# Gated linear attention and max-out MoE on one core: weights w2 and w_out loaded ahead of unit 0, w1 ahead of unit 1, unit 2 loaded by halves

## The chip, the core and the metric

The kernel runs on one core of a Trainium2 chip. The time is the device time of one launch in microseconds (us). It is the median of several executions; the profile comes from one further execution and is read beside its own time.

## What is computed

```python
def _attn_ref(q, k, v, alpha):                    # (4, 8, 768, 48) each
    B, H, S, D = q.shape
    state = np.zeros((B, H, D, D), dtype=np.float32)
    y = np.zeros_like(q)
    for t in range(S):
        state = alpha[:, :, t, :, None] * state + np.einsum('bhd,bhe->bhde', k[:, :, t], v[:, :, t])
        y[:, :, t] = np.einsum('bhd,bhde->bhe', q[:, :, t], state)
    return y

def _moe_ref(x, w1, w2, w_out):                   # x (3072, 384), w1, w2 (384, 1024), w_out (1024, 384)
    h1 = x @ w1
    h2 = x @ w2
    g = np.maximum(h1, h2)
    return g @ w_out

x = np.ascontiguousarray(attn_out.transpose(0, 2, 1, 3)).reshape(B * S, H * D)
out = _moe_ref(x, w1, w2, w_out)
```

A recurrent attention with a decay alpha per step, head and channel, and then a layer that takes the larger of two projections and projects back. Inputs and output are float32; the kernel multiplies in float16.

## The kernel before

**Units.** The sequence of 768 is cut into 6 chunks of 128 steps, the batch of 4 into 2 groups of two. A unit is one chunk of one group: 12 units, 0 to 11, with unit u chunk u // 2 of group u % 2. Inside a unit, `bb` is 0 or 1, one half for each of the two batch entries. The state goes from unit u - 2 to unit u, so units 0 and 1 have none to take in.

**What one unit does.** `ln(u)`: logarithm of alpha, on ACT. `sums(u)`: prefix sums of it by matmuls, on PE. `exps(u)`: five exponentials on ACT (Em and cs for each half, then the decay de). `kmul(u, bb)` on POOL and `qmul(u, bb)` on DVE scale k and q; `vcast` on POOL casts v to float16; `scale(u, bb)` is these three. `turn(u, bb)`: transposes of k and q on PE, copied as qk by DVE. `kv`: the chunk's own contribution to the state, matmuls and DVE copies or additions into tm. `pairs(u, bb)`: the 128x128 products of q and k, which DVE masks into pt, two instructions a half. Then the attention output: for units 0 and 1 `yfirst` and `xfirst` by halves (matmul, ACT copy xn, transposes, DVE copy xt), for later units `ystate`, `yin` and `xturn`.

**The MoE.** max(x w1, x w2) is computed as relu(x (w1 - w2)) + x w2. `wsub(n)` forms a quarter of w1 - w2 on DVE; `hid(u, f2)`, f2 = 0 to 3, multiplies x by it and takes the relu (ACT for f2 = 0, 1, 2, DVE for 3) into gT; `outp(u, n)` multiplies gT by w_out and adds x times the product w2 w_out. That product w2o is made once: `wturn(ds)` transposes w2, `wcast(n)` casts half of w_out (ACT and POOL), `wmul(n)` multiplies, `wout()` copies the three results out of PSUM.

**Order.** The schedule is manual: each engine runs its instructions in the order in which the program calls these functions, and the semaphores between them are put in by the framework. All input loads are issued on the SP queue in program order; a unit's loads are alpha (two DMAs) and k, q, v (one DMA each for both halves, or one for each half). The framework hands eight DMA semaphores round, so that a DMA is issued after an earlier one on the same semaphore, as a rule the eighth before it, has landed. Outputs are issued on the ACT queue. The load buffers (`ldp`, 4 deep) hold four units.

**The head.** Lines 424 to 508 write out units 0 and 1, the preparation of the weights and the start of unit 2 by hand; `dummies(n)` issues n matmuls whose result is not used. From `for u in range(2, NU)` on, a loop runs the remaining units, with MoE u - 1 among the steps of unit u and the scaling of unit u + 1. Before, the head in order: loads of unit 0's alpha and first half, w2, unit 0's second half, w_out, alpha of unit 1, w1, the rest of unit 1; unit 0 runs while w2 is turned; the product w2 w_out comes after unit 0's second half; then `wsub` and MoE 0 (`hid(0, *)`) among the scaling of unit 1, and MoE 1 with only scaling and `turn` of unit 2.

**PSUM.** Buffers by tag: "g" (4 buffers) for sums, transposes and attention, "pp" (2) for pairs, "m" (2) for hid, outp, the w2 transposes and the dummies; the product w2 w_out uses both pp buffers and one g buffer until `wout`.

Of the kernel before, what the change touches and what calls it, by code (L numbers as in the profile page):

```python
# [15 lines left out]
def kernel(  # L16
# [22 lines left out]
    nc = tc.nc  # L39
# [23 lines left out]
    def load_alpha(u):  # L63
        c, g = divmod(u, NG)
        t = st.setdefault(u, {})
        t["af"] = ldp.tile([128, H, 2, D], FP32, tag="af", name="af")
        for bb in range(2):
            nc.sync.dma_start(  # L68
                out=t["af"][64 * bb : 64 * bb + 64],
                in_=alpha[2 * g + bb, :, c * C : (c + 1) * C, :].rearrange("h (p j) d -> p h (j d)", j=2),  # L70
            )

    def load_kqv(u, bbs):
        c, g = divmod(u, NG)
        t = st[u]
        for name, src in (("kf", k), ("qf", q), ("vf", v)):
            if name not in t:
                t[name] = ldp.tile([128, 2, H, D], FP32, tag=name, name=name)
            lo, hi = bbs[0], bbs[-1] + 1
            nc.sync.dma_start(  # L80
                out=t[name][:, lo:hi].rearrange("p b h d -> p (b h) d"),
                in_=src[2 * g + lo : 2 * g + hi, :, c * C : (c + 1) * C, :].rearrange("b h p d -> p (b h) d"),
            )

    def load(u):
        load_alpha(u)
        load_kqv(u, (0, 1))
# [1 line left out]
    w2f = wp.tile([128, ND, DFF], FP32)  # L89
    wof = wp.tile([128, NF, DM], FP32)  # L90
    w1f = wp.tile([128, ND, DFF], FP32)
    load_alpha(0)
    load_kqv(0, (0,))
    for ds in range(ND):
        nc.sync.dma_start(out=w2f[:, ds], in_=moe_w2[ds * 128 : (ds + 1) * 128])
    load_kqv(0, (1,))
    for n in range(2):
        f = slice(n * NF // 2, (n + 1) * NF // 2)
        nc.sync.dma_start(out=wof[:, f], in_=moe_w_out.rearrange("(s p) d -> p s d", p=128)[:, f])
    load_alpha(1)  # L100
    for n in range(4):
        f = slice(n * DFF // 4, (n + 1) * DFF // 4)
        nc.sync.dma_start(out=w1f[:, :, f], in_=moe_w1.rearrange("(s p) f -> p s f", p=128)[:, :, f])  # L103
    load_kqv(1, (0,))
    load_kqv(1, (1,))

    wz = constp.tile([128, 512], FP16)
    nc.vector.memset(wz, 0.0)
# [48 lines left out]
    def ln(u):  # L157
        X = st[u]
        X["lg"] = LG[u % NB]
        nc.scalar.activation(  # L160
            out=X["lg"][:, :, :, 0:D], in_=X["af"].rearrange("p h j d -> p j h d"), func=ACTF.Ln
        )
# [8 lines left out]
    def sums(u):  # L171
        X = st[u]
        c, g = divmod(u, NG)
        lg = X["lg"]
        cs = [new("g", [128, 512], FP32, 4, "cs") for _ in range(2)]
        X["csv"] = csv = [x[:, 0 : H * D].rearrange("p (h d) -> p h d", h=H) for x in cs]
        dps = cs[0][:, H * D : H * D + 4 * HP].rearrange("p (j b n) -> p j b n", j=HP, b=2)
        for hp in range(HP):
            for j in range(2):
                nc.tensor.matmul(  # L180
                    dps[:, hp], lhsT=pair(lg[:, j], hp), rhs=halves, start=(j == 0), stop=(j == 1)
                )
        for j in range(2):
            for bb in range(2):
                r = slice(64 * bb, 64 * bb + 64)
                nc.tensor.matmul(csv[bb], lhsT=mc[r, j], rhs=lg[r, j, :, 0:D], start=(j == 0), stop=(j == 1))  # L186
        X["dps"] = dps
        X["qn"], X["kn"], X["Em"] = [], [], []
        for bb in range(2):
            X["qn"].append(QN[(2 * u + bb) % (2 * NB)])  # L190
            X["kn"].append(KN[(2 * u + bb) % (2 * NB)])
# [17 lines left out]
    def exps(u):  # L209
        for bb in range(2):  # L210
            expm(u, bb)
            expp(u, bb)
        expd(u)
# [57 lines left out]
    def pairs(u, bb):  # L271
        X = st[u]
        qk = X["qk", bb]
        pt = X["pt", bb] = gp.tile([128, 2, HP, C], FP16, tag="pt", name="pt")
        pa = [new("pp", [128, HP, C], FP32, 2, "pp") for _ in range(2)]
        for j in range(HP):
            for a in range(2):
                r = slice(64 * a, 64 * a + D)
                nc.tensor.matmul(pa[a][:, j, :], lhsT=qk[r, 1, j, :], rhs=qk[r, 0, j, :], start=True, stop=True)  # L279
        for a in range(2):  # L280
            nc.vector.tensor_mul(out=pt[:, a], in0=pa[a], in1=u16.unsqueeze(1).to_broadcast([128, HP, C]))  # L281
# [40 lines left out]
    def yfirst(u, bb):  # L322

        X = st[u]
        ya = new("g", [128, H, D], FP32, 4, "yb")
        for h in range(H):
            nc.tensor.matmul(
                ya[:, h, :], lhsT=X["pt", bb][:, h % 2, h // 2, :], rhs=X["v16"][:, bb, h, :], start=True, stop=True
            )
        if bb == 0:  # L330
            X["xn"] = gp.tile([128, 2, HP, 2, D], FP16, tag="xn", name="xn")
            X["xt"] = mp.tile([128, ND, 2, C], FP16, tag="xt", bufs=3, name="xt")
        nc.scalar.copy(out=X["xn"][:, bb].rearrange("p j a d -> p (j a) d"), in_=ya)

    def xfirst(u, bb):
        X = st[u]
        xp = new("g", [128, ND, C], FP16, 4, "xb")
        xf = X["xn"][:, bb].rearrange("p j a d -> p (j a d)")
        for ds in range(ND):
            nc.tensor.transpose(xp[:, ds, :], xf[:, ds * 128 : (ds + 1) * 128], ident)  # L340
        nc.vector.tensor_copy(out=X["xt"][:, :, bb, :], in_=xp)
# [38 lines left out]
    def wturn(ds):  # L380
        wt = new("m", [128, NF, 128], FP16, 2, "wt")
        for f in range(NF):
            nc.tensor.transpose(wt[:, f, :], w2h[:, ds, f * 128 : (f + 1) * 128], ident)
        nc.vector.tensor_copy(out=w2T[:, :, ds * 128 : (ds + 1) * 128], in_=wt)
# [13 lines left out]

    def wout():
        for ds in range(ND):  # L400
            nc.scalar.copy(out=w2o[:, ds, :], in_=wqs[ds])

    def wcast(n):
        nc.scalar.copy(out=wo16[:, 4 * n : 4 * n + 2], in_=wof[:, 4 * n : 4 * n + 2])
        nc.gpsimd.tensor_copy(out=wo16[:, 4 * n + 2 : 4 * n + 4], in_=wof[:, 4 * n + 2 : 4 * n + 4])
# [7 lines left out]
    def dummies(n):  # L413
        warm = new("m", [128, 512], FP32, 2, "warm")
        for _ in range(n):
            nc.tensor.matmul(warm, lhsT=wz[:, 0:128], rhs=wz, start=True, stop=True)  # L416
# [5 lines left out]


    dummies(10)
    ln(0)
    sums(0)
    exps(0)
    dummies(6)
    scale(0, 0)
    for ds in range(ND):  # L430
        nc.scalar.copy(out=w2h[:, ds, :], in_=w2f[:, ds, :])
    turn(0, 0)
    kv(0, (0,))
    dummies(2)
    pairs(0, 0)
    dummies(2)
    wturn(0)
    yfirst(0, 0)
    dummies(2)
    wturn(1)  # L440
    dummies(2)
    xfirst(0, 0)
    wturn(2)
    scale(0, 1)
    dummies(2)
    turn(0, 1)
    kv(0, (1,))
    dummies(3)
    pairs(0, 1)
    load(2)  # L450
    dummies(6)
    wcast(0)
    yfirst(0, 1)
    wmul(0)
    xfirst(0, 1)
    wcast(1)
    wmul(1)
    ln(1)
    wout()

    sums(1)
    load(3)
    wsub(0)
    wsub(1)
    hid(0, 0)
    expm(1, 0)
    hid(0, 1)
    expp(1, 0)
    wsub(2)
    wsub(3)  # L470
    hid(0, 2)
    expm(1, 1)
    expp(1, 1)
    scale(1, 0)
    hid(0, 3)
    expd(1)
    turn(1, 0)
    kv(1, (0,))
    outp(0, 0)
    scale(1, 1)  # L480
    pairs(1, 0)
    load(4)
    turn(1, 1)
    kv(1, (1,))
    yfirst(1, 0)
    outp(0, 1)
    pairs(1, 1)
    ln(2)
    xfirst(1, 0)
    sums(2)  # L490
    dummies(2)
    yfirst(1, 1)
    exps(2)
    dummies(2)
    xfirst(1, 1)
    for bb in range(2):
        kmul(2, bb)
    state(2)
    vcast(2)
    for bb in range(2):  # L500
        qmul(2, bb)
    hid(1, 0)
    hid(1, 1)
    turn(2, 0)
    hid(1, 2)
    turn(2, 1)
    hid(1, 3)
    load(5)


    for u in range(2, NU):
        nxt = u + 1 < NU
        pairs(u, 0)
        kv(u)
        if nxt:
            ln(u + 1)
        if u > 2:
            hid(u - 1, 0)
            hid(u - 1, 1)
        else:  # L520
            outp(1, 0)
        if nxt:
            sums(u + 1)
            exps(u + 1)
            for bb in range(2):
                kmul(u + 1, bb)
            state(u + 1)
            vcast(u + 1)
        pairs(u, 1)
        if u > 2:  # L530
            hid(u - 1, 2)
        ystate(u)
        if u > 2:
            hid(u - 1, 3)
        if nxt:
            for bb in range(2):
                qmul(u + 1, bb)
        yin(u)
        outp(u - 1, 0 if u > 2 else 1)
        if nxt:  # L540
            turn(u + 1, 0)
        xturn(u)
        if nxt:
            turn(u + 1, 1)
        if u > 2:
            outp(u - 1, 1)
        if u + 4 < NU:
            load(u + 4)
# [34 lines left out]
```

## Time and profile before

| what | us |
|---|---|
| median of 13 runs | 155.21 |
| lowest, highest | 154.23, 157.5 |
| the profiled execution's own time | 155.68 |
| its span, first to last instruction | 154.0 |
| PE busy, share of the span | 140.9 (92%) |
| DVE, ACT, POOL busy | 93.2, 78.7, 47.5 |
| mean rate of all DMA | 186 GB/s, 28.58 MB |
| mean granted clock of PE | 0.986 |

The profiled execution is 0.47 us longer than the median. PE, DVE, ACT and POOL are the matmul, vector, scalar and GpSimd engines; PEld is the weight load of PE. SP only issues DMAs. A busy PE is a modelled end of pipelined matmuls. In a timeline row, "idle before" is the time for which that engine had nothing running, and the name behind it is the instruction or DMA whose semaphore came last. A wait that is put down to an engine can be one for something older.

### The profile page before, as it was taken

How to read it: one execution, taken by the hardware profiler on the slowest of the kernel's cores; microseconds unless marked ns; L12 is line 12 of the kernel's file. 1: busy time of each engine (PE TensorE's matmuls, PEld its weight loads, DVE VectorE, ACT ScalarE, POOL GpSimd, SP SyncE). 2: the span in 40 equal slices, each digit the busy share in tenths (PEclk: the TensorE clock that was granted, in tenths of full speed). 3: DMA queues.
4: the chain of work that ended last, by engine and by line, in shares of the span. 5: the costliest groups of instructions: out<-in, count | busy, mean ns of one | idle time of the engine just before them, and what ended most of it. 6: DMA issues, size and time to landing. Idle time of an engine off the chain costs nothing.

```text
span 154.0 us, 4086 instructions
## 1 busy us (share of the span) xinstructions
PE 140.9 (92%) x1671; PEld 96.7 (63%) x1671; DVE 93.2 (61%) x192; ACT 78.7 (51%) x165; POOL 47.5 (31%) x73
## 2 busy tenths in 40 slices
PE   6878898777799899999999999999999999999991
PEld 2236354344376687777777777777767767767660
DVE  5057816675259699495786775866858575753010
ACT  3365137712563668285392762944918629244421
POOL 6032320330080717227054090360721805400000
PEclk9999999999779999999999999999999999999998
DMA  3999999999999799999999999999998952020202
GB/s 82 199 381 218 366 229 321 172 206 171 236 201 185 155 198 219 196 231 223 168 261 189 236 206 194 238 187 196 234 185 193 235 100 98 4 102 4 97 5 102
DMA packets 93459, 28.58 MB, mean 186 GB/s; under 512 B 87424, under 2 KB 93056, under 8 KB 93440
## 3 DMA queue, kind: packets, MB, share of 16 engines
q1 hardware_dynamic: 90160, 23.60, 85.1%
q10 hardware_dynamic: 3280, 4.72, 8.6%
q8 instruction: 13, 0.21, 0.7%
q14 instruction: 6, 0.05, 0.1%
HBM read 23.59 MB, written 4.72 MB: 184 GB/s over the span
## 4 chain that ended last, share of the span: by engine, by line
PE 70%; SPq 18%; DMA 3%; ACT 3%; issue 2%; ACTq 1%; DVE 1%; POOL 0%
PE op L370 19%; PE hp L352 19%; SPq L80 10%; PE op L368 8%; PE tp L243 6%; SPq L103 4%; PE pp L279 4%; DMA vf<-in_v_dram 3%; PE cs L186 3%; PE kv L259 3%; PE ya L303 3%; PE xp L318 2%; SPq L68 2%; PE ya L291 2%; PE cs L180 1%
## 5 line engine op out<-in xcount | busy, mean ns | idle before, releaser
L232 POOL TENSOR_TENSOR kn<-kf,Em 128x384 f16<-128x384 f32 x24 | 23.5, 998 | 74.8 <-ACT Em L197 63.0
L352 PE MATMUL hp<-xt,w 128*128 128x256 f16 x288 | 38.2, 276 | 1.9 <-DVE w L409 1.2
L281 DVE TENSOR_TENSOR pt<-pp,u 128x512 f16<-128x512 f32 x48 | 30.9, 686 | 13.4 <-PE pp L279 13.0
L370 PE MATMUL op<-wo,gT 128*128 128x384 f16 x192 | 35.1, 326 | 0.0
L373 ACT COPY outs<-op 128x384 f32<-128x384 f32 x24 | 11.5, 479 | 42.8 <-PE op L370 42.8
L352 PEld LDWEIGHTS <-w 128*128 128x128 f16 x288 | 26.1, 99 | 8.0 <-DVE w L409 2.4
L370 PEld LDWEIGHTS <-gT 128*128 128x128 f16 x192 | 18.8, 98 | 12.4
L245 DVE COPY qk<-tp 128x1024 f16<-128x1024 f16 x24 | 16.5, 687 | 12.5 <-PE tp L243 12.5
L357 ACT ACTIVATE gT<-hp 128x512 f16<-128x512 f32 x36 | 20.6, 594 | 5.3 <-PE hp L352 4.9
L236 DVE TENSOR_TENSOR qn<-qf,cs 128x384 f16<-128x384 f32 x24 | 12.3, 548 | 7.9 <-ACT de L207 6.5
L368 PE MATMUL op<-w2o,xt 128*128 128x384 f16 x72 | 15.6, 325 | 0.0
L160 ACT ACTIVATE lg<-af 128x768 f16<-128x768 f32 x12 | 10.1, 842 | 9.7 <-DMA af<-in_alpha_dram 5.5
L416 PE MATMUL warm<-wz 128*128 128x512 f16 x39 | 12.8, 458 | 1.3 <-DVE halves L123 1.3
L359 DVE TENSOR_SCALAR gT<-hp 128x512 f16<-128x512 f32 x12 | 8.3, 691 | 8.2 <-PE hp L352 8.2
L197 ACT ACTIVATE Em<-cs 128x384 f32<-128x384 f32 x24 | 11.7, 488 | 1.1 <-PE cs L186 1.1
L202 ACT ACTIVATE cs<-cs 128x384 f32<-128x384 f32 x24 | 11.8, 491 | 0.0
L169 POOL CAST v<-vf 128x768 f16<-128x768 f32 (+1 forms) x14 | 10.3, 733 | 4.4 <-DMA vf<-in_v_dram 4.4
L267 DVE TENSOR_TENSOR tm<-kv,sb 64x192 f32<-64x192 f32 x32 | 11.3, 353 | 0.5
L243 PE MATMUL tp<-ident,qn 128*128 128x128 f16 x96 | 9.3, 219 | 1.1 <-DVE qn L236 1.0
L279 PEld LDWEIGHTS <-qk 48*128 48x128 f16 x192 | 6.2, 94 | 6.1 <-issue 3.1
L243 PE MATMUL tp<-ident,kn 128*128 128x128 f16 x96 | 9.3, 219 | 0.5 <-POOL kn L232 0.5
L279 PE MATMUL pp<-qk 48*128 48x128 f16 x192 | 9.5, 217 | 0.2 <-DVE qk L245 0.2
(57 smaller groups left out, 143.3 us busy)
## 6 DMA issues: line engine op xcount, KB each, us to landing
af<-in_alpha_dram SPq DMA_DIRECT2D x24, 192.0 KB, 5.7
out_dram<-outs ACTq DMA_DIRECT2D x11, 384.0 KB, 4.2
kf<-in_k_dram SPq DMA_DIRECT2D x10, 384.0 KB, 6.3
qf<-in_q_dram SPq DMA_DIRECT2D x10, 384.0 KB, 7.5
vf<-in_v_dram SPq DMA_DIRECT2D x10, 384.0 KB, 7.0
w2f<-in_moe_w_dram SPq DMA_DIRECT2D x3, 512.0 KB, 5.2
wof<-in_moe_w_out_dram SPq DMA_DIRECT2D x2, 768.0 KB, 7.2
w1f<-in_moe_w_dram SPq DMA_DIRECT2D x4, 384.0 KB, 8.5
```

What stands on the lines that cost most here:

```text
L80: nc.sync.dma_start(out=t[name][:, lo:hi].rearrange("p b h d -> p (b h) d"), in_=src[2 * g + lo : 2 * g + hi, :, c * C : (c + 1) * C, :].r ...
L232: nc.gpsimd.tensor_mul(out=X["kn"][bb][:, :, 0:D], in0=X["kf"][:, bb], in1=X["Em"][bb])
L236: nc.vector.tensor_mul(out=X["qn"][bb][:, :, 0:D], in0=X["qf"][:, bb], in1=X["csv"][bb])
L243: nc.tensor.transpose(tp[:, n, j, :], pair(src, j), ident)
L245: nc.vector.tensor_copy(out=qk, in_=tp)
L279: nc.tensor.matmul(pa[a][:, j, :], lhsT=qk[r, 1, j, :], rhs=qk[r, 0, j, :], start=True, stop=True)
L281: nc.vector.tensor_mul(out=pt[:, a], in0=pa[a], in1=u16.unsqueeze(1).to_broadcast([128, HP, C]))
L352: nc.tensor.matmul(hp[:, n, :], lhsT=w12[:, ds, f * 128 : (f + 1) * 128], rhs=X["xt"][:, ds].rearrange("p n t -> p (n t)"), start=(ds == 0 ...
L357: nc.scalar.activation(out=gT[:, 2 * f2 : 2 * f2 + 2, :], in_=hp, func=ACTF.Relu)
L368: nc.tensor.matmul(op, lhsT=X["xt"][:, ds, n, :], rhs=w2o[:, ds, :], start=(ds == 0), stop=False)
L370: nc.tensor.matmul(op, lhsT=X["gT"][:, f, n * C : (n + 1) * C], rhs=wo16[:, f, :], start=False, stop=(f == NF - 1))
L416: nc.tensor.matmul(warm, lhsT=wz[:, 0:128], rhs=wz, start=True, stop=True)
```

## The change

The loads at the top are put in another order: w2, w_out, all of unit 0 (by halves), w1, then units 1 and 2, both by halves; `load(2)` in the head goes. `wout` moves from ACT to DVE. In the head the preparation of w2 and w_out stands ahead of unit 0; the `wsub` quarters stand in unit 0's second half and MoE 0; `ln`, `sums` and `exps` of unit 1 follow MoE 0's relus; `yfirst(1, 1)` comes ahead of `sums(2)`; unit 2's `vcast` is split, and its first `pairs`, its second `qmul` and its `kv` stand inside MoE 1. Dummies are placed anew, 39 in all before and after. The loop is the same but for unit 2's `pairs(u, 0)` and `kv(u)`, which it leaves out.

```diff
--- before.py
+++ after.py
@@ -89,20 +89,21 @@
     w2f = wp.tile([128, ND, DFF], FP32)
     wof = wp.tile([128, NF, DM], FP32)
     w1f = wp.tile([128, ND, DFF], FP32)
-    load_alpha(0)
-    load_kqv(0, (0,))
     for ds in range(ND):
         nc.sync.dma_start(out=w2f[:, ds], in_=moe_w2[ds * 128 : (ds + 1) * 128])
-    load_kqv(0, (1,))
     for n in range(2):
         f = slice(n * NF // 2, (n + 1) * NF // 2)
         nc.sync.dma_start(out=wof[:, f], in_=moe_w_out.rearrange("(s p) d -> p s d", p=128)[:, f])
-    load_alpha(1)
+    load_alpha(0)
+    load_kqv(0, (0,))
+    load_kqv(0, (1,))
     for n in range(4):
         f = slice(n * DFF // 4, (n + 1) * DFF // 4)
         nc.sync.dma_start(out=w1f[:, :, f], in_=moe_w1.rearrange("(s p) f -> p s f", p=128)[:, :, f])
-    load_kqv(1, (0,))
-    load_kqv(1, (1,))
+    for u in (1, 2):
+        load_alpha(u)
+        load_kqv(u, (0,))
+        load_kqv(u, (1,))
 
     wz = constp.tile([128, 512], FP16)
     nc.vector.memset(wz, 0.0)
@@ -398,7 +399,7 @@
 
     def wout():
         for ds in range(ND):
-            nc.scalar.copy(out=w2o[:, ds, :], in_=wqs[ds])
+            nc.vector.tensor_copy(out=w2o[:, ds, :], in_=wqs[ds])
 
     def wcast(n):
         nc.scalar.copy(out=wo16[:, 4 * n : 4 * n + 2], in_=wof[:, 4 * n : 4 * n + 2])
@@ -422,96 +423,91 @@
 
 
     dummies(10)
+    for ds in range(ND):
+        nc.scalar.copy(out=w2h[:, ds, :], in_=w2f[:, ds, :])
+        wturn(ds)
+        dummies(2)
+    wcast(0)
+    wmul(0)
+    wcast(1)
+    wmul(1)
     ln(0)
     sums(0)
+    wout()
     exps(0)
-    dummies(6)
+    dummies(4)
     scale(0, 0)
-    for ds in range(ND):
-        nc.scalar.copy(out=w2h[:, ds, :], in_=w2f[:, ds, :])
     turn(0, 0)
     kv(0, (0,))
     dummies(2)
     pairs(0, 0)
-    dummies(2)
-    wturn(0)
-    yfirst(0, 0)
-    dummies(2)
-    wturn(1)
-    dummies(2)
-    xfirst(0, 0)
-    wturn(2)
     scale(0, 1)
     dummies(2)
     turn(0, 1)
     kv(0, (1,))
+    yfirst(0, 0)
+    dummies(2)
+    pairs(0, 1)
+    xfirst(0, 0)
+    wsub(0)
+    dummies(5)
+    yfirst(0, 1)
+    wsub(1)
     dummies(3)
-    pairs(0, 1)
-    load(2)
-    dummies(6)
-    wcast(0)
-    yfirst(0, 1)
-    wmul(0)
     xfirst(0, 1)
-    wcast(1)
-    wmul(1)
+
+    load(3)
+    hid(0, 0)
+    wsub(2)
+    hid(0, 1)
+    wsub(3)
     ln(1)
-    wout()
-
+    hid(0, 2)
+    hid(0, 3)
     sums(1)
-    load(3)
-    wsub(0)
-    wsub(1)
-    hid(0, 0)
-    expm(1, 0)
-    hid(0, 1)
-    expp(1, 0)
-    wsub(2)
-    wsub(3)
-    hid(0, 2)
-    expm(1, 1)
-    expp(1, 1)
+    exps(1)
+    outp(0, 0)
     scale(1, 0)
-    hid(0, 3)
-    expd(1)
     turn(1, 0)
     kv(1, (0,))
-    outp(0, 0)
+    outp(0, 1)
     scale(1, 1)
     pairs(1, 0)
     load(4)
     turn(1, 1)
     kv(1, (1,))
     yfirst(1, 0)
-    outp(0, 1)
     pairs(1, 1)
     ln(2)
     xfirst(1, 0)
+    dummies(3)
+    yfirst(1, 1)
     sums(2)
-    dummies(2)
-    yfirst(1, 1)
     exps(2)
     dummies(2)
     xfirst(1, 1)
     for bb in range(2):
         kmul(2, bb)
+        vcast(2, (bb,))
     state(2)
-    vcast(2)
-    for bb in range(2):
-        qmul(2, bb)
+    qmul(2, 0)
     hid(1, 0)
     hid(1, 1)
     turn(2, 0)
     hid(1, 2)
+    pairs(2, 0)
+    qmul(2, 1)
     turn(2, 1)
     hid(1, 3)
+    kv(2)
     load(5)
 
 
     for u in range(2, NU):
         nxt = u + 1 < NU
-        pairs(u, 0)
-        kv(u)
+        if u > 2:
+            pairs(u, 0)
+            kv(u)
         if nxt:
             ln(u + 1)
         if u > 2:
```

## The prediction

> **What bounds the kernel now.** I read the page's slices first. From slice 12 (46 us) on the matmul engine is 9 or more tenths busy; later periods are 10.07 us apart (the 12 matmuls of hp start at 55.66, 65.71, 75.78 us) and hold almost no gap. The change ends before that loop, so what counts is when its steady part begins. Before it the DMA row is full while PE is not, and the chain of waits is nearly all SP queue up to 29 us.
>
> ```profile
> PE   6878898777799899999999999999999999999991
> DMA  3999999999999799999999999999998952020202
> GB/s 82 199 381 218 366 229 321 172 206 171 236 201 185 155 198 219 196 231 223 168 261 189 236 206 194 238 187 196 234 185 193 235 100 98 4 102 4 97 5 102
> ```
>
> Next the timeline of the head: who starts at which landing. Columns: start, duration, engine, line, tiles, and in brackets the idle time and who ended it.
>
> ```profile
> 5.40 0.84 ACT L160 ACTIVATE lg<-af 128x768 f16<-128x768 f32 x1 [3.32 <-DMA af<-in_alpha_dram]
> 9.85 1.05 ACT L431 CAST w2h<-w2f 128x1024 f16<-128x1024 f32 x1 [0.96 <-DMA w2f<-in_moe_w_dram]
> 12.59 1.05 ACT L431 CAST w2h<-w2f 128x1024 f16<-128x1024 f32 x1 [0.42 <-DMA w2f<-in_moe_w_dram]
> 15.49 0.50 POOL L169 CAST v<-vf 128x384 f16<-128x384 f32 x1 [0.73 <-DMA vf<-in_v_dram]
> 18.53 0.83 ACT L404 CAST wo<-wof 128x768 f16<-128x768 f32 x1 [4.52 <-DMA wof<-in_moe_w_out_dram]
> 21.21 0.83 ACT L404 CAST wo<-wof 128x768 f16<-128x768 f32 x1 [0.98 <-DMA wof<-in_moe_w_out_dram]
> 23.34 0.84 ACT L160 ACTIVATE lg<-af 128x768 f16<-128x768 f32 x1 [1.30 <-DMA af<-in_alpha_dram]
> 25.33 0.83 PE L352 MATMUL hp<-xt,w 128*128 128x256 f16 x6 [0.31 <-DVE w L409]
> 34.45 0.51 POOL L169 CAST v<-vf 128x384 f16<-128x384 f32 x1 [2.00 <-DMA vf<-in_v_dram]
> 42.63 2.07 PE L352 MATMUL hp<-xt,w 128*128 128x256 f16 x12 [0.45 <-DVE xt L341]
> 47.52 0.65 PE L368 MATMUL op<-w2o,xt 128*128 128x384 f16 x3
> ```
>
> Each bracket is a landing: unit 0's alpha at 5.4, w2 done at 12.6, unit 0 done at 15.5, w_out at 18.5 and 21.2, unit 1's alpha 23.3, w1 24.3 to 27.7, unit 1's last v 34.4. MoE 0 begins at 25.33, MoE 1 at 42.63, and outp(1,0), from which on both kernels do the same, at 47.52. Last the granted clock in stretches of 3.41 us (columns: stretch, its length, PE busy, matmuls, clock, DMA share, GB/s):
>
> ```profile
> 26.83:30.24 3.41, 2.42 (x20) 1.00 1.01 169
> 33.65:37.07 3.42, 2.41 (x30) 1.00 1.08 154
> 37.07:40.48 3.41, 2.01 (x27) 1.00 0.99 177
> 40.48:43.89 3.41, 2.96 (x21) 0.50 1.22 289
> ```
>
> A stretch with 2.01 us of matmul is followed by one at half clock, one with 2.41 is not. Half clock cost 1.0 us here: two dummies took 1.03 us where others take 0.59 (0.4 more), and 12 hp matmuls 2.07 where they take 1.47 (0.6).
>
> **The change, step by step.** The bytes are the same; the order is new. I walk it from start to outp(1,0), with durations from these rows.
>
> *Loads.* Alpha 0 (two transfers) was in at 5.40, kqv transfers are 1.0 apart, so the first w2 piece, of 1.4 (9.85 to 12.59 is two), lands at 5.4 - 2 x 1.0 + 1.4 = 4.8, the third at 7.6. A w_out half: by the landings 2.9 ((21.21 - 15.49) / 2); by the rate in the slices that held large packets (366 to 381 GB/s, 786 KB) 2.1. I take 2.4: 10.0 and 12.4; ends 11.8 and 13.3. Alpha 0 follows 2.1 later (21.21 to 23.34): 14.5. Unit 0's six kqv, 1.05 each, end at 20.8, w1 (4 x 1.2) at 25.5, alpha 1 at 27.6, the time at which w1 ended before; unit 1 lands as before, up to 34.4.
>
> *w2 and w_out.* Casts 1.05 and transposes follow each landing. wcast(1) 0.83 after 12.4, wmul(1) 2.11: 15.4. ln(0) is behind the casts on ACT, ends 14.5 + 0.84 = 15.3; sums(0) is behind wmul(1) on PE: 15.4 (ends 14.6, 16.2). Before, sums(0) was at 6.30: this 9.1 us is what moving it past w2 and w_out costs.
>
> *wout on DVE.* No row has this copy. Bounds: 0.36 (128x384 f16 from PSUM, L341) and 0.69 (128x512 f32, L359); 0.5, three 1.5, in place of 1.22 on ACT. DVE has nothing to do from 15.4 until qmul(0,0) at 18.0, so nothing; without that cover all 1.5 would delay unit 0. The Trainium skill ("Advanced Engine Details and Errata", The Read-Write Bubble) says ScalarE is nearer to PSUM, VectorE to SBUF; by that rule the move loses, by the rows 0.3 us, under cover either way.
>
> *Unit 0.* sums(0) to the end of pt(0,0) took 6.30 to 12.61 = 6.3: 21.7. In DVE's order qmul(0,1) stands behind it (0.5: 22.2), then q's transposes and the qk copy (1.2, as 16.18 to 17.36: 23.4), tm 0.6, the two pt 1.3: 25.3; xt(0,0) 0.3: 25.6. wsub(0) and wsub(1) (1.99 for two) stand ahead of xt(0,1): 27.5, then 0.35 more, and MoE 0 starts at 27.8, against 25.33: 2.5 late. xfirst(0,1) alone would be in by 26.8 (pt 25.3, yb 0.4, xn 0.5, xb 0.35, dummies beside them), so the wsubs cost 0.6 of it.
>
> *MoE 0, unit 1.* w1 is there: the waits of 0.2 to 0.4 before each hp group go, the buffers set the pace. hp to relu 0.87 + 0.60: hid(0,2) at 29.3, hid(0,3) 29.95; ln(1) 0.84 lies between relus, sums(1) 30.7, Em 31.55, de ends 1.76 later (7.12 to 8.88): 33.3. qmul 0.55, transposes, kv: 34.4; outp(0,1) 1.8: 36.2; pairs(1,0) 0.4, its pt 1.3: 37.85; qk(1,1) 0.6, tm 0.7: 39.1; pt(1,1) 1.25: 40.3. Nothing waits for unit 1's v (34.4) any more. yfirst(1,1) now stands ahead of sums(2): 40.7; xn 0.5, sums(2), two dummies and xb: 42.0; xt 0.4. MoE 1 at 42.45, against 42.63. So 2.3 of the 2.5 us come back. exps(2) ends at 43.1.
>
> *Unit 2 in MoE 1.* qmul(2,0) 43.7, hid(1,0) and (1,1) 1.31: 43.75; transposes 0.45; hid(1,2) 0.65; qk copied at 44.9; pairs(2,0) 45.0 to 45.35; pt(2,0) 1.3: 46.65. qmul(2,1) is now behind pt(2,0) on DVE: 47.15. turn(2,1) is ahead of hid(1,3) and kv(2) on PE and needs it, so PE stands from 45.5 to 47.2: a new wait of 1.65, with all of PE behind it. Then 0.2 + 0.65 + 0.45: outp(1,0) at 48.55, against 47.52. **Sum: 1.05 later.** In exchange pairs(2,0) and kv(2) are done, but before they also were by 47.52.
>
> *The rest, at nothing.* SP issues six halves for unit 2, where there were three: 3 x 0.6 us of SP, under landings of 1 us each. load(3) waits for the DMA eight earlier on its semaphores, now out 0 (issued about 37, landed 5 us later), so alpha 3 lands up to 1.5 later than before; ln(3) had it before 46.3 and sums(3) needs it at 50.4. If that cover went, at most the rest of 1.5 shows. vcast(2) in two casts costs POOL 2 x 0.50 - 0.82, in a POOL idle 69% of the span. Same dummies in all (39).
>
> *The clock.* With the stall, 43.9 to 47.3 holds about 1.6 us of matmul, less than the 2.01 that was followed by half clock. Where the stretches begin can differ by run; a stretch with 1.2 us or more of this gap begins in 2.7 of 3.41 us. Half clock then falls on hid(1,3) to outp(1,0), dense matmuls: between 0 (no drop) and 1.7 (half of 3.41). I take what it cost before, 1.0.
> The Trainium skill ("TensorE: Matmul & The Clock Gate", Part 1: The HAM clock gate) states that the clock falls after a whole idle window of some 3.4 us; by it a gap of 1.65 does nothing, which leaves 1.0 out of the sum. The row of 37.07 disagrees: its longest gap was 1.40.
>
> The profiled execution took 155.68 (span 154.0 and 1.7 around it), 0.47 over the median 155.21. 155.68 + 1.05 + 1.0 = 157.7, less 0.47: **157.2**.
>
> **Rivals.**
> *No drop of the clock* (the gap falls across two stretches, or 1.6 is enough activity): 155.68 + 1.05 - 0.47 = 156.2. For: in 0.7 of 3.41 us of phases; the 2.41 rows kept the clock. Against: 2.01 lost it.
> *Not slower: the weights stream at packet rate.* Place: the 3.1 MB at the head. If w_out takes 2.1 a half, wmul(1) ends at 14.8, alpha 0 is in at 13.7 or, with 0.8 a piece instead of 1.05 at its start, sums(0) is at 14.5, 0.9 earlier, and as unit 0 and 1 are a chain of latencies, all of it moves: 155.3 with the clock kept, and faster if a few of the 40 steps also overlap better. It decides from w_out landing at 11.7 or earlier. For: 366 to 381 GB/s. Against: landings 3.0 and 2.7 apart though the same slices held them, and it needs the clock kept.
> *Later still.* Weights land as before (2.9 a half): sums(0) 16.2, 0.8 more; or the idle PE of unit 0 (some 2.1 to 2.4 us of matmul in 16.6 to 20.0 and 20.0 to 23.4) halves the clock there too, 0.5 to 1.0. 158.3.
> *Hidden anyway:* if unit 1's v set everything, the head would not matter; but in the walk it is not waited for.
>
> **How the numbers follow.** Forecast 157.2: 0.45. Clock kept, 156.2: 0.27. Weights at packet rate, 155.3: 0.18. Later, 158.3: 0.10. 0.3% is 0.47 us (about what a measurement here can tell): faster is below 154.74, same up to 155.68. Each case carries some 0.6 either way. Faster gets most of the lower half of the third, 0.12; same its upper half and a tail of the second, 0.13; slower 0.75. Range: down to 154.9, which leaves 0.13 below, up to 158.6, 0.06 above.
>
> **What would show it.** sums(0) at 15.4 +- 0.8; hp's first group at 27.8; MoE 1 near 42.5; L237 for the second half of unit 2 behind two pt, PE idle some 1.6 us before its transposes, outp(1,0) near 48.6; half clock in the 3.4 us after it. Wrong, if PE does not stand there, if MoE 0 starts before 26.5 or if the loop's period is no longer 10.07.

## The result and the profile after

The changed kernel takes 158.22 us (median of 11 runs, 156.54 to 161.01), the kernel before 155.38 (48 runs, 154.23 to 157.5). The ratio is 1.014, 95% interval 1.0104 to 1.0176: slower by 1.4%. The ratio leaves out the longest runs (of the changed kernel the four of 159 us and more, in which the matmul clock was lowered for a time), the median 158.22 does not; 1.014 x 155.38 is 157.6. The profiled execution of the changed kernel took 156.76 us with a span of 155.0, and its clock was never lowered; that of before took 155.68 with a span of 154.0.

The page of after, its slices (tenths of 40 equal parts of the span):

```profile
PE   6878667998778899999999999999999999999990
PEclk9999999999999999999999999999999999999999
DMA  5999999899899898999999999999998952020202
```

PE is full from slice 14 on (54 us; slices are counted from 0), as before, whose slice 13 holds 8 tenths too, and the steady loop still needs 10.06 to 10.13 us a unit; most of what was lost was lost ahead of it. DMA is full from the first slices on, in either order. The clock row has no dip.

Where unit 0 now begins, on ACT of after (start, duration, engine, line, operation; in brackets the idle time and who ended it):

```profile
7.17 1.04 ACT L427 CAST w2h<-w2f 128x1024 f16<-128x1024 f32 x1 [0.24 <-DMA w2f<-in_moe_w_dram]
9.29 0.83 ACT L405 CAST wo<-wof 128x768 f16<-128x768 f32 x1 [1.07 <-DMA wof<-in_moe_w_out_dram]
12.08 0.83 ACT L405 CAST wo<-wof 128x768 f16<-128x768 f32 x1 [1.96 <-DMA wof<-in_moe_w_out_dram]
14.11 0.84 ACT L161 ACTIVATE lg<-af 128x768 f16<-128x768 f32 x1 [1.20 <-DMA af<-in_alpha_dram]
```

The brackets are landings: w2 is in at 7.17, w_out at 9.29 and 12.08, unit 0's alpha at 14.11 (before: 12.6, 18.5 and 21.2, 5.4). Then PE of after:

```profile
12.96 2.11 PE L395 MATMUL wq<-wo,w2T 128*128 128x384 f16 x12 [0.68 <-ACT wo L405]
15.01 0.35 PE L181 MATMUL cs<-halves,lg 128*128 128x4 f16 x8
27.22 2.97 PE L353 MATMUL hp<-xt,w 128*128 128x256 f16 x24 [1.00 <-DVE xt L342]
42.06 1.47 PE L353 MATMUL hp<-xt,w 128*128 128x256 f16 x12 [0.45 <-DVE xt L342]
47.00 0.40 PE L244 MATMUL tp<-ident,qn 128*128 128x128 f16 x4 [1.51 <-DVE qn L237]
47.23 0.82 PE L353 MATMUL hp<-xt,w 128*128 128x256 f16 x6
48.23 0.65 PE L369 MATMUL op<-w2o,xt 128*128 128x384 f16 x3
```

sums(0) is at 15.01 (before 6.30), MoE 0 at 27.22 (25.33), MoE 1 at 42.06 (42.63). MoE 0's 24 matmuls are now one row without a wait inside; w1 is there. Inside MoE 1 stands a new wait of 1.51 us ahead of q's transposes, and outp(1,0) is at 48.23 (47.52). DVE of after says why:

```profile
45.19 1.29 DVE L282 TENSOR_TENSOR pt<-pp,u 128x512 f16<-128x512 f32 x2 [0.49 <-PE pp L280]
46.40 0.54 DVE L237 TENSOR_TENSOR qn<-qf,cs 128x384 f16<-128x384 f32 x1
```

qmul(2,1) has no bracket: its inputs were ready, and it stood in DVE's queue behind the two pt of pairs(2,0).

### The profile page after: what moved, and what is told of

It is laid out like the page before. It is cut to its first block, busy times and chain, and to the rows that moved or that the text cites. A ratio compares the mean times of both kernels' runs of the same rounds, so it can differ in the third digit from the quotient of the medians.

```text
span 155.0 us, 4092 instructions
## 1 busy us (share of the span) xinstructions
PE 139.6 (90%) x1671; PEld 96.3 (62%) x1671; DVE 94.7 (61%) x195; ACT 77.6 (50%) x162; POOL 47.4 (31%) x74
## 4 chain that ended last, share of the span: by engine, by line
PE 73%; DVE 10%; DMA 6%; ACT 5%; issue 2%; SPq 1%; ACTq 1%
PE hp L353 20%; PE op L371 19%; PE op L369 8%; PE tp L244 7%; DMA wof<-in_moe_w_out_dram 6%; DVE pt L282 4%; PE pp L280 4%; PE cs L187 3%; PE ya L304 2%; PE kv L260 2%; PE xp L319 2%; PE cs L181 2%; PE ya L292 2%; DVE qk L246 2%; PE wq L395 1%
## 5 line engine op out<-in xcount | busy, mean ns | idle before, releaser
L353 PE MATMUL hp<-xt,w 128*128 128x256 f16 x288 | 37.3, 273 | 1.8 <-DVE xt L342 1.5
L282 DVE TENSOR_TENSOR pt<-pp,u 128x512 f16<-128x512 f32 x48 | 30.9, 686 | 13.0 <-PE pp L280 12.7
L417 PE MATMUL warm<-wz 128*128 128x512 f16 x39 | 12.2, 435 | 1.3 <-DVE halves L124 1.3
L198 ACT ACTIVATE Em<-cs 128x384 f32<-128x384 f32 x24 | 11.7, 488 | 1.7 <-PE cs L187 1.6
L203 ACT ACTIVATE cs<-cs 128x384 f32<-128x384 f32 x24 | 11.7, 490 | 0.0
```

What stands on the lines that cost most here:

```text
L198: nc.scalar.activation(out=Em, in_=X["csv"][bb], func=ACTF.Exp, scale=-1.0)
L353: nc.tensor.matmul(hp[:, n, :], lhsT=w12[:, ds, f * 128 : (f + 1) * 128], rhs=X["xt"][:, ds].rearrange("p n t -> p (n t)"), start=(ds == 0 ...
```

## The experiments

Twelve kernels were run. The ratio is to the kernel before on the same chip, with its 95% interval; "sums(0)", "MoE 1" and "outp(1,0)" are starts in the kernel's profile (that of e5_half_wout has a lowered clock).

| kernel | ratio | interval | sums(0) | MoE 1 | outp(1,0) | span less sums(0) |
|---|---|---|---|---|---|---|
| after | 1.014 | 1.0104 to 1.0176 | 15.01 | 42.06 | 48.23 | 140.0 |
| e1_qmul_first | 1.0104 | 1.0055 to 1.0152 | 15.21 | 42.27 | 46.76 | 138.2 |
| e2_fill_stall | 1.016 | 1.0094 to 1.0226 | 14.59 | 41.65 | 47.81 | 139.9 |
| e3_head_alone | 1.0074 | 1.0039 to 1.0109 | 16.34 | 43.40 | 47.69 | 138.0 |
| e4_moe1_alone | 1.0141 | 1.0091 to 1.019 | 6.32 | 42.68 | 48.84 | |
| e5_half_wout | 1.0021 | 0.9982 to 1.0061 | 17.93 | 44.96 | 49.44 | 138.1 |
| e6_wsub_pool | 1.0089 | 1.0048 to 1.0129 | 14.72 | 41.22 | 45.71 | 138.6 |
| e7_fill_unit0 | 1.011 | 1.0069 to 1.0152 | 17.18 | 44.23 | 48.52 | 138.1 |
| e8_yfirst_before | 1.0005 | 0.9975 to 1.0034 | 7.02 | 41.74 | 46.03 | |
| e9_fill_head | 1.0124 | 1.0078 to 1.017 | 14.80 | 42.27 | 46.75 | 139.1 |
| e10_before_kv_late | 1.0001 | 0.9976 to 1.0027 | 6.44 | 41.56 | 45.84 | |
| e11_after_kv_late | 1.0057 | 1.0017 to 1.0097 | 14.58 | 41.20 | 45.69 | 138.3 |
| e12_ln_late | 0.9972 | 0.9946 to 0.9997 | 6.33 | 40.56 | 44.85 | |

**The stall taken away.** Only the place of qmul(2,1) changes.

```diff
     qmul(2, 0)
+    qmul(2, 1)
     hid(1, 0)
...
     pairs(2, 0)
-    qmul(2, 1)
     turn(2, 1)
```

> The changed kernel with one line moved: unit 2's second qmul stands ahead of hid(1,0), so on DVE ahead of pt(2,0). Theory of the stall: PE no longer stands 1.5 us before the second transposes of unit 2; hid(1,3) at 45.6 and outp(1,0) at 46.6 instead of 48.23; the profiled time falls by 1.5 to some 155.2, the median to 155 to 156. Rival, the wait only moves (DVE still has to do pt(2,0), qk, relu and tm, and PE then waits for gT(1,3) or pt(2,1)): less than 0.5 is gained. Rival, the loss sits in the head (loads, unit 0): no change, a median near 158.

The profiled execution took 155.16 us, as the theory had it; the median of the six runs, 156.30, is above its 155 to 156. PE of e1_qmul_first in the same place:

```profile
42.27 1.47 PE L353 MATMUL hp<-xt,w 128*128 128x256 f16 x12 [0.45 <-DVE xt L342]
45.54 0.39 PE L244 MATMUL tp<-ident,qn 128*128 128x128 f16 x4
45.76 0.82 PE L353 MATMUL hp<-xt,w 128*128 128x256 f16 x6
46.76 0.49 PE L369 MATMUL op<-w2o,xt 128*128 128x384 f16 x2
```

q's transposes have no bracket any more. From MoE 1 to outp(1,0) it is 4.49 us in place of 6.17, and from sums(0) to the end 138.2 in place of 140.0. So in these profiles the place of one DVE instruction behind another costs 1.8 us: the 1.51, and some tenths behind it. The ratios, 1.0104 and 1.014, have intervals that overlap: six runs do not tell these two kernels apart by time.

**The stall filled.** Six dummies stand ahead of turn(2,1), to see whether the stall costs more than itself, by way of the clock.

```diff
     qmul(2, 1)
+    dummies(6)
     turn(2, 1)
```

> The changed kernel with six dummies ahead of turn(2,1), about 1.3 us of PE inside the wait of 1.5; the wait itself stays. Theory that the idle PE of this wait costs the clock in a part of the executions: mean clocks go to 0.99 to 1.0 in nearly all, the median falls by 0.7 to 1.5, to about 157, and the long executions of 159 to 161 are gone. Rival, the clock falls in the idle stretches of unit 0: clocks of 0.96 to 0.99 remain and the median stays at 158 to 158.5.

The wait is filled, outp(1,0) still comes 6.16 us behind MoE 1, and the ratio, 1.016, is no better than that of after. The long executions stay, 160.20 and 160.40 us with clocks of 0.974 and 0.975, and so does the median, 158.25: the theory's numbers fail, the rival's come true, though no profile shows its cause. None of the six runs has a mean clock between 0.98 and 0.995, the mark of one lowered stretch of 3.41 us; three of six runs of e4_moe1_alone have, with the same stall open (0.989 each, 157.18 to 158.04 us, where its other three took 156.01 to 156.98), and two of after's twelve. The kernel before, which has no stall, has such a clock in 19 of 86 runs, so these counts do not show that the stall brings the drop that the prediction counted on, and the median is not made of it.

**The two halves of the change by themselves.** e3_head_alone has the new head and MoE 1 as before; e4_moe1_alone is the kernel before with only unit 2's pieces put into MoE 1 (and its `pairs(u, 0)` and `kv(u)` left out of the loop, not shown):

```diff
-    for bb in range(2):
-        qmul(2, bb)
+    qmul(2, 0)
     hid(1, 0)
...
     hid(1, 2)
+    pairs(2, 0)
+    qmul(2, 1)
     turn(2, 1)
     hid(1, 3)
+    kv(2)
```

> The changed kernel with MoE 1 and unit 2 as before (one vcast, both qmul first, pairs and kv of unit 2 in the loop): the head of the change alone. Theory of the stall: MoE 1 begins at 42.1 as in the changed kernel, no wait of 1.5, outp(1,0) near 46.4, the profiled time some 155.0, the median 155 to 156, about that of before. Rival, the head is what costs: 156.5 to 158.

> The kernel before with only the other part: unit 2's first pairs, second qmul behind it and kv inside MoE 1, loads and unit 0 untouched (unit 2's load and vcast stay whole). Theory of the stall: PE stands 1.4 to 1.7 us ahead of the second transposes of unit 2, and the time is 1.0 to 1.5 over before, 156.4 to 157. Rival, the head is what costs: within 0.3 of before.

Each is slower by itself: the head 1.0074, MoE 1 1.0141. For the head neither expectation holds: MoE 1 begins at 43.40, not 42.1, and the median, 156.12 us, lies between the theory's 155 to 156 and the rival's 156.5 to 158. The stall in e4_moe1_alone is again 1.51 us (q's transposes at 47.62). The two shares add up to more than the whole, 1.0215 against 1.014; with intervals of 0.35 and 0.5% that is not much, and the head's share hangs on when the weights land. The profiles show this: sums(0) ranges from 14.58 to 17.18 us over the eight that kept their clock, and the second half of w_out landed between 11.40 and 14.33 us. In after, e1, e2, e3 and e7 MoE 1 then follows 27.05 or 27.06 us behind sums(0), though the landings in between differ. Unit 0 to MoE 1 is a chain of fixed length that starts when w_out is in and multiplied, unless a later load is late: in e9, where unit 1's alpha landed at 29.34 us (28.47 in after), sums(1) waited 0.35 for it and MoE 1 came 27.47 behind sums(0). e1 and e3 are 138.2 and 138.0 from sums(0) to the end: without the stall, unit 2's pieces inside MoE 1 bring nothing either.

**Half of w_out.** The second half of w_out is not loaded; the first half's data are used twice. Edit to e1_qmul_first:

```diff
-    for n in range(2):
+    for n in range(1):
```

> The kernel of e1_qmul_first with the second half of w_out left out: it isn't loaded, its casts read the first half again (as much casting and multiplying as before, other numbers). In the four profiles so far the span less the start of sums(0) is 139.9 to 140.0 with the wait in MoE 1 and 138.1 to 138.2 without. Theory that unit 0 is a chain that hangs on the landing of w_out: nothing waits for a second half, sums(0) starts at 14.4 (wcast(0) after the first half at 9.3, both wmul in a row), the span is 152.5, and the median falls by 1.5 to 2, to 154.3 to 154.8. Rival, later loads (unit 0's k, q, v, unit 1's v) set the end in the longer executions: the median falls by less than 0.5, or the difference of span and sums(0) grows.

The ratio falls from 1.0104 to 1.0021: 0.79 MB less ahead of unit 0 takes back some 1.3 us of the 1.6 that e1 had lost. That fits a chain that hangs on the load of w_out, but it is less than was expected: the median is 155.72 us, not 154.3 to 154.8, and the two intervals just meet. The profile was taken in a run with a lowered clock, and it shows where that was. Windows of e5_half_wout (stretch; its length, PE busy, matmuls; clock; DMA share; GB/s):

```profile
5.95:9.36 3.41, 2.12 (x23) 1.00 1.09 336
9.36:12.77 3.41, 1.20 (x12) 1.00 1.18 158
12.77:16.18 3.41, 3.41 (x13) 0.50 0.84 165
16.18:19.59 3.41, 3.41 (x28) 1.00 0.99 249
```

In this run the one half of w_out landed at 11.45 us, where after's first half landed at 9.27; PE stood for 2.21 us, and the clock fell for wmul, whose 24 matmuls took 5.74 us.

**The wsubs off DVE.** The prediction put 0.6 us of MoE 0's start down to two wsubs ahead of xt(0,1). In e1_qmul_first, three of four go to POOL.

```diff
-        nc.vector.tensor_sub(out=w12[:, :, f], in0=w1f[:, :, f], in1=w2f[:, :, f])
+        eng = nc.vector if n == 3 else nc.gpsimd
+        eng.tensor_sub(out=w12[:, :, f], in0=w1f[:, :, f], in1=w2f[:, :, f])
```

> The kernel of e1_qmul_first with the first three quarters of w1 - w2 on POOL, which has nothing to do from 20.6 to 31.5 us, in place of DVE. Theory that the two wsubs ahead of xt(0,1) cost 0.6: MoE 0 starts 11.6 after sums(0) in place of 12.2, and all that follows 0.6 earlier; the time falls by 0.3 to 0.6. Rival, a subtraction on POOL takes 2 us or more a quarter (kn, half as large, takes 1.0) and hid(0,1) or hid(0,2) waits for it: nothing is gained.

sums(0) to MoE 0 is 11.66 us in place of 12.22, the 0.56 that was priced; a wsub takes 1.8 us on POOL and 0.9 on DVE, under cover. outp(1,0) is at 45.71, 1.05 earlier than in e1, of which 0.49 comes from the earlier sums(0). But the span is only 0.1 shorter. PE of e6_wsub_pool, the start of sums(4):

```profile
54.07 1.47 PE L353 MATMUL hp<-xt,w 128*128 128x256 f16 x12
55.99 0.18 PE L181 MATMUL cs<-halves,lg 128*128 128x4 f16 x1 [0.44 <-ACT lg L161]
```

A wait that neither before nor after has: for unit 4's alpha. What was gained by 45 us is gone by 56.

**Unit 0's idle PE filled.** Ten dummies more in e3_head_alone's unit 0.

```diff
     exps(0)
-    dummies(4)
+    dummies(6)
...
     scale(0, 1)
-    dummies(2)
+    dummies(6)
...
     xfirst(0, 1)
+    dummies(4)
```

> The kernel of e3_head_alone with ten more dummies in the idle stretches of PE in unit 0 (two ahead of turn(0,0), four ahead of turn(0,1), four ahead of hid(0,0)). Theory that these stretches cost the clock in the executions with a mean clock of 0.974 to 0.978 (two of twelve in e3_head_alone): none below 0.985, the median 155.5 to 156. Rival, the clock comes late at the start or falls elsewhere: such executions remain, 156.1 as e3_head_alone.

1.011 against 1.0074: no gain. None of its six runs has a mean clock under 0.98; of e3's twelve two have. In six runs that is too few to show anything.

**The kernel before with one step of the change.** yfirst(1,1) ahead of sums(2), as the change has it, with three dummies in place of two, and nothing else.

```diff
+    dummies(3)
+    yfirst(1, 1)
     sums(2)
-    dummies(2)
-    yfirst(1, 1)
     exps(2)
```

> The kernel before with one part of the change alone: yfirst(1,1) ahead of sums(2), three dummies between xfirst(1,0) and it. Theory: in the kernel before, yfirst(1,1) had its pt at 38.98 and waited for sums(2), that is for ln(2), until 40.49; ahead of it, MoE 1 starts 0.9 to 1.3 earlier (41.3 to 41.7), the time falls by 0.6 to 1.2 to about 153.8. Rival, exps(2) sets MoE 1's pace (its relus stand behind it on ACT) or the clock still falls: less than 0.3.

outp(1,0) comes at 46.03, 1.5 us earlier than in the profile of before (1.0 of it is the half clock that the profile of before happened to have), and the time stays: 1.0005. PE of e8_yfirst_before:

```profile
54.15 0.50 PE L259 MATMUL kv<-v,kn 128*128 128x96 f16 x8 [0.26 <-POOL v L169]
54.48 1.47 PE L352 MATMUL hp<-xt,w 128*128 128x256 f16 x12
56.58 0.35 PE L180 MATMUL cs<-halves,lg 128*128 128x4 f16 x8 [0.62 <-ACT lg L160]
```

Again 0.88 us for unit 3's v and unit 4's alpha. The second alpha transfer of unit 4 landed at 54.34 in before, 55.00 in after, 55.06 in e6 and 55.60 in e8: the stream of loads gets there at about the same time whatever the order at its start. Until then DMA has no slack; sums(4) cannot be much ahead of 56, and before had it at 56.97 with its clock lowered for 3.41 us on the way. One thing did change: none of the twelve runs of e8 has a clock under 0.99, and with e10 and e12 below it is 2 of 36, against 20 of 86 of before. The three dummies stand in the stretch that came ahead of before's drop. The time did not fall all the same.

**The head's waits filled.** With the drop of e5 in mind, eight dummies more while e1_qmul_first waits for its weights.

```diff
         wturn(ds)
-        dummies(2)
+        dummies((2, 4, 6)[ds])
     wcast(0)
     wmul(0)
     wcast(1)
+    dummies(2)
     wmul(1)
```

> The kernel of e1_qmul_first with eight dummies more while the head waits for its weights (four and six in place of two behind the second and the third w2 turn, two ahead of wmul(1)). The profile of e5_half_wout was taken in a run with one half-clock stretch, 12.77 to 16.18 us, and the stretch before it (9.36 to 12.77) held 1.20 us of matmuls and an idle piece of 2.21 us, the wait for w_out. Theory: the lower mean clocks (0.979 and less) that one run in five of every kernel with the changed head had come from this wait, in the runs in which a weight lands late. Then none of this kernel's runs has a mean clock under 0.98, its slowest run is under 157.5 us (e1_qmul_first had 159.2), and its ratio to the kernel before is 1.005 to 1.010, with sums(0) 0 to 0.4 us later than the 15.2 us of e1_qmul_first. Rival: the clock falls elsewhere (unit 0, or whatever the loads do); then one run in five again has 0.98 or less and takes over 158 us.

The theory's number fails: 1.0124, and one run of six has a clock of 0.978 (158.96 us). That is the rival's one in five, but six runs cannot tell one in six from none, and a late w_out would outlast the dummies. Where the lower clocks come from stays open, but for the one stretch that e5 caught.

**Work put into the wait for the loads.** e10 is e8, e11 is e6, with kv(3) and hid(2,2) moved, in unit 3 alone; e12 moves ln(4) in e10 as well (shown together):

```diff
-        kv(u)
-        if nxt:
+        if u != 3:
+            kv(u)
+        if nxt and u != 3:
             ln(u + 1)
         if u > 2:
             hid(u - 1, 0)
             hid(u - 1, 1)
+            if u == 3:
+                ln(u + 1)
+                kv(u)
+                hid(u - 1, 2)
...
         pairs(u, 1)
-        if u > 2:
+        if u > 3:
             hid(u - 1, 2)
```

> The kernel of e8_yfirst_before, in which in unit 3 alone kv(3) moves behind hid(2,1) and hid(2,2) ahead of sums(4). e8_yfirst_before had outp(1,0) at 46.03 us against 47.52 before, but the next two-unit step took 13.73 in place of 12.61 us: PE waited 0.26 us for unit 3's v at kv(3) and 0.62 us at sums(4) for unit 4's alpha, both of which had just landed. Theory: the stream of loads has no slack in either order, and whatever the head gains is lost there, some 12 us later; work put into that wait gives it back. Then outp(2,0) moves from 13.73 to about 12.9 us behind outp(1,0), and the time is 154.0 to 154.4 us, ratio 0.994 to 0.997. Rival: the wait only moves to the next unit, whose alpha lands late too (64.89 us in e8_yfirst_before against sums(5) at about 66); then the time stays at 154.8 to 155.2 us, ratio 0.998 to 1.002, with a new wait at sums(5).

> The kernel of e6_wsub_pool (the change with qmul(2,1) early and three wsubs on POOL) with the same move in unit 3: kv(3) behind hid(2,1), hid(2,2) ahead of sums(4). e6_wsub_pool had outp(1,0) at 45.71 us, 1.05 earlier than e1_qmul_first, but the next step took 13.46 in place of 12.61, with 0.44 us of waiting for unit 4's alpha at sums(4). Theory of the stream without slack: the step is 12.7 to 13.0 us and the time 155.6 to 156.1 us, ratio 1.004 to 1.008 (lower where the clock holds). Rival (the wait moves on to sums(5)): as e6_wsub_pool, 156.3 to 156.7 us, ratio about 1.009.

e10 missed: 1.0001, the step from outp(1,0) to outp(2,0) 13.82 us. The wait had not gone to sums(5), as the rival had it, but into ACT's queue. PE and then ACT of e10_before_kv_late:

```profile
56.52 0.81 PE L352 MATMUL hp<-xt,w 128*128 128x256 f16 x6 [0.94 <-ACT gT L357]
```

```profile
55.14 0.84 ACT L160 ACTIVATE lg<-af 128x768 f16<-128x768 f32 x1 [2.55 <-DMA af<-in_alpha_dram]
55.89 1.07 ACT L357 ACTIVATE gT<-hp 128x512 f16<-128x512 f32 x2
```

ln(4) waits for alpha at the head of ACT's queue and holds up the relus behind it, whose buffers hid(2,2) needs. In e11 the same move leaves 0.22 there; its step is 13.09 us against 13.46, where 12.7 to 13.0 was expected, and its ratio is 1.0057.

> The kernel of e10_before_kv_late with ln(4) moved behind hid(2,1) as well. There the wait had gone over to ACT's queue: ln(4) stood in it ahead of hid(2,0)'s gT and waited for unit 4's alpha until 55.14 us, gT ran at 55.89, and PE waited 0.94 us ahead of hid(2,2), which needs the buffer that gT frees; outp(2,0) came 13.82 us behind outp(1,0). Theory (the stream of loads has no slack, and work put into the wait gives it back): gT of hid(2,0) and hid(2,1) run at 54.5 to 55.7, ln(4) from about 55.7 to 56.6, sums(4) at 56.4 to 56.7 behind hid(2,2); the step is 13.0 to 13.3 us, and the time 154.2 to 154.6 us, ratio 0.995 to 0.998. Rival: alpha 4 lands late enough in most runs, or the wait goes on to sums(5), so that the step shrinks and the next one grows by as much: 154.9 to 155.3 us, ratio 0.999 to 1.002.

PE and ACT of e12_ln_late:

```profile
54.41 0.82 PE L352 MATMUL hp<-xt,w 128*128 128x256 f16 x6
55.66 0.35 PE L180 MATMUL cs<-halves,lg 128*128 128x4 f16 x8 [0.43 <-ACT lg L160]
```

```profile
53.62 1.25 ACT L357 ACTIVATE gT<-hp 128x512 f16<-128x512 f32 x2 [2.03 <-PE hp L352]
54.77 0.83 ACT L160 ACTIVATE lg<-af 128x768 f16<-128x768 f32 x1
```

The step is 13.32 us, 0.5 shorter than e10's and just past the 13.0 to 13.3 expected, and the time 154.33 us against 154.98 before, ratio 0.9972 (0.9946 to 0.9997). It is the one kernel of the study that beats both, by 0.3%, and the interval ends close to one. Its head is that of before but for yfirst(1,1).

## Why the prediction was right

**The order of the head: right.** sums(0) was forecast at 15.4 and came at 15.01, MoE 0 at 27.8 and 27.22, MoE 1 at 42.45 and 42.06, each 0.4 to 0.6 early because the third w2 piece and w_out landed 0.3 to 0.7 sooner than worked out. The three w2o copies on DVE took 1.86 us where 1.5 was taken (1.22 on ACT before), under the cover that was named: DVE then stood for 1.95 us. Two wsubs ahead of xt(0,1) were priced at 0.6, and moving them gave 0.56.

**The stall: right.** "qmul(2,1) is now behind pt(2,0) on DVE" was forecast to make PE wait 1.65 us from 45.5; it waited 1.51 until 47.00, and moving that one instruction away removed it. The sum of these parts, 155.68 + 1.05 = 156.73, stands beside the profiled execution's 156.76, but that close only by luck: outp(1,0) came 0.71 late, not 1.05. Another 0.09 us was lost in the loop up to the last outp, and 0.27 at the very end, which the prediction had at nothing. The last copy of before and of after:

```profile
150.75 0.48 ACT L373 COPY outs<-op 128x384 f32<-128x384 f32 x1 [1.31 <-PE op L370]
151.55 0.48 ACT L374 COPY outs<-op 128x384 f32<-128x384 f32 x1 [1.31 <-PE op L371]
```

From there to the end of the span (153.97 and 155.05 us) it is 2.75 us in before and 3.02 in after. In the traces SP ends the program by waiting for the DMA semaphores one after the other, some 0.065 us each. In before the last output lands on the one that SP takes last; in after, with three DMAs more, on one that has four behind it. Every kernel with the loads of before has 2.74 to 2.75 us there, every one with the new loads 3.01 to 3.02, and e5, with one DMA fewer, 2.92.

**The clock: wrong, in both profiles.** The step was "Half clock then falls on hid(1,3) to outp(1,0) ... I take what it cost before, 1.0." In after's profile the clock did not fall there. The clock record of its trace puts the bounds of the stretches at 42.51, 45.92 and 49.33 us, so the idle time, 45.49 to 47.00, fell across two of them (windows of after):

```profile
42.51:45.92 3.41, 2.85 (x36) 1.00 0.94 183
45.92:49.33 3.41, 2.33 (x25) 1.00 1.45 189
```

That is the condition under which the prediction's first rival, at 0.27, kept the clock. In e4_moe1_alone the stall lies across two stretches as well; no profile has it inside one, so whether it then costs the clock was not seen. The profile of before, though, had such a drop, and 155.68 holds its cost of 1.0 us; the sum should have been made against an execution without it. The kernel's runs bear this out: of 86 runs of before beside the experiments, the 66 with a mean clock of 0.99 or more have a median of 154.72 us, and the 19 with 0.98 to 0.99 one of 155.53. The prediction did not keep to one base: its "So 2.3 of the 2.5 us come back" comes out only against a MoE 1 at 42.23, which is 42.63 less the 0.4 of the half clock, while its 1.05 is counted from 47.52, with the half clock in it. So the change costs about 2.0 us at full clock by the profiled execution (156.76 - 154.72), 2.2 by the median of the seven runs of after with 0.99 or more (156.96). That is the size of the +1.05 and +1.0 of the forecast, but the second term is right by luck: it was put down to a drop in after that did not come, and made up for one in before that had been overlooked. Taking 0.47 off because the profiled execution was over the median then made 157.2 a little low: 157.6 by the ratio.

The rule behind that step was read from one row and does not hold up. Before's profile lost its clock after a stretch with 2.01 us of matmuls; after kept it after 1.98 (windows of after):

```profile
18.61:22.03 3.42, 1.98 (x25) 1.00 1.04 310
22.03:25.44 3.41, 3.23 (x44) 1.00 1.20 275
```

and e3_head_alone after 1.73; e5's 1.20 lost it. The Trainium skill ("TensorE: Matmul & The Clock Gate", Part 1: The HAM clock gate) has the clock fall after a whole idle window of some 3.4 us; two drops here followed stretches that were busy for 1.20 and 2.01 us, so the runs do not bear that out as a bound either. What decides between 1.2 and 2.0 us stays open.

**The rivals.** "Weights stream at packet rate" asked for w_out in by 11.7 us. It was: in e2_fill_stall, which is after with dummies in the stall, it landed at 11.40, and sums(0) came at 14.59, the rival's 14.5. Its profiled execution still took 156.19 us, 1.5 over the full-clock median of before: too little is gained there. What all cases of the prediction left out is the load of unit 4. The walk ended at outp(1,0), "from which on both kernels do the same". They do the same, but an outp(1,0) ahead of some 46.5 us is not kept, since unit 4's alpha lands at 54.2 to 56.6 us in all profiles but that of e5 (56.9), whatever the order. e1, at 46.76, still kept what it had gained on after; e6 and e8, at 45.71 and 46.03, waited. Without its drop before would stand at about 46.5 itself (47.52 less 1.0, an estimate), so there was little for any order of the head to gain.

**Where the time went.** In the profiles 1.8 us hang on the stall (from sums(0) to the end, e1 against after) and 0.27 on the end of the program. The rest is the head, whose chain now starts with w_out's landing, 9 us later, and gets most of it back by MoE 1; how much depends on that landing. Against a span of before without its drop (153.97 less 1.0, an estimate), and with the 0.27 taken off, the kernels without the stall are 0.2 us longer in e1, 1.1 in e3 and 2.0 in e7, where w_out was in at 11.91, 13.43 and 14.33 us. The run times give the stall less: 1.014 and 1.016 with it, 1.0074 to 1.0124 in the kernels with the new head and without it (e1, e3, e7, e9), about 0.5% or 0.8 us. One way in which the rest goes stands in e9's profile: outp(1,0) at 46.75, then 0.23 us of waiting at sums(4), and a step of 13.03 us to outp(2,0) in place of after's 12.62. That most runs without the stall lose it in this way was not shown, nor was when w_out landed in the runs that were not profiled.

## What to carry to other kernels

Loading in another order moves what waits, not the sum: ask first when the last load before the steady loop lands; here no order of the head gained anything past that, and only work moved into the wait itself (e12) gained 0.3%. Before an instruction is put behind another in an engine's queue, see who waits for it; here one multiplication of 0.54 us behind two masks stopped the matmul engine for 1.5 us, and later a logarithm that waited for its load stopped relus that were ready. Check whether the profiled execution itself had a lowered clock before a sum is made against it. And look at the end of the program too: here three DMAs more put the last output on an earlier semaphore, and that cost 0.27 us whatever the schedule did.

## What the runs showed that was not expected

The landing of the same weights in the same order varied by almost 3 us between executions: w_out's second half at 11.40 to 14.33 us in eight profiles. Mean clocks of 0.98 and less, two or three lowered stretches of 3.41 us, came in 13 of the 84 runs with the changed head (0.963 to 0.978, 157.9 to 161.0 us), in one of the 86 runs of before, and in none of the 42 of e4, e8, e10 and e12, which have its loads. So they come with the new loads or head; what triggers them was not caught in a profile. The same subtraction took 1.8 us on POOL and 0.9 on DVE.
